# A gated scan with top-128 expert rows: loads and stores by units of both halves, plain transposes, a shared weighing

## The chip, the cores and the metric

The kernel runs on one core of one Trainium2 chip. The metric is device time in microseconds (us) of one execution. The kernel before takes 238.24 us in the median of three runs (237.73 to 239.63). The profile was taken in another execution of 240.62 us.

A core has five engines that work side by side: PE (matrix products and transposes; "PEld" is its loading of the stationary operand), DVE (VectorE), ACT (ScalarE), POOL (GpSimd) and SP, which here issues transfers. Sixteen DMA engines move data between HBM and the on-chip memory SBUF; PE writes its results into PSUM.

## What is computed

For each of 4 batches, a sequence of 6208 steps with 256 channels goes through a gated recurrence; then the 128 rows with the highest score get an expert's output added.

```python
sig = 1.0 / (1.0 + np.exp(-f_logit))
f = lower_bound + (1.0 - lower_bound) * sig
i = 1.0 - f
for t in range(S):
    h = f[:, t] * h + i[:, t] * x[:, t]
    y[:, t] = h
...
scores = np.einsum('bsd,d->bs', y, w_gate)
out = y.copy()
for b in range(B):
    top_idx = np.argpartition(-scores[b], capacity)[:capacity]
    xe = y[b, top_idx]
    h = np.maximum(xe @ w1, 0.0)
    ye = h @ w2
    g = 1.0 / (1.0 + np.exp(-scores[b, top_idx]))
    out[b, top_idx] = xe + g[:, None] * ye
```

B, S, D, F = 4, 6208, 256, 1024; capacity is 128; all data are float32.

## The kernel before

The host hands over x and f_logit transposed, as (batch, channel, step). The 256 channels are two halves of 128 partitions. A batch is cut into 24 blocks of 256 steps after a tail of 64 steps; blocks are grouped into units of four (UNITS; the last batch ends in units of 3 and 1). The work item is a half of a unit, `half(s)`, 50 in all, mostly 128 partitions by 1024 steps:

- `load_f` (L247) and `load_x` (L251): one transfer each on SP, 512 KB, a run of 4 KB per partition. There are 6 f buffers and 10 x buffers.
- `gate` on ACT (L261): sigmoid of -f_logit, that is (1 - sig). `forget` on ACT (L275): 1 - (1 - lower_bound) x gate, into a PSUM tile `gt` of which there are two. Where a unit has the tail, its 64 columns go through extra small instructions (L259, L274).
- `prepare` on POOL (L278), for the second half only: x times (1 - lower_bound). `weigh` on POOL (L282): x times gate. For the first two and the last two halves ("direct") DVE weighs in one instruction (L285).
- `scan` on DVE (L293): the recurrence, in place in x, multiply and add.
- `scores` on PE (L301): the scan times w_gate into one PSUM bank, by a matrix that puts each block on its own partition.
- `turn` on PE: transposes of 128 steps by 128 channels. The first half goes by a product with a diagonal matrix that also multiplies by (1 - lower_bound) (L307); the second half by a plain transpose (L309). Four go into one PSUM tile `pt`, of which there are two. `put` on ACT (L329) copies them to the row tile `ym`.
- `store` on SP (L332), once both halves of a unit are there: 1 MB, in runs of 2 rows = 2 KB. There are 10 `ym` buffers.

After a batch's last scores comes a search for the 128 rows (`choose`): `keep` copies the scores from PSUM (L388), `lanes` (L393) spreads them on PE over 32 partitions of a PSUM bank `acc`, `top` to `ranks` on DVE (L401 to L428) find and rank candidates, `pull` (L439) collects the row numbers, `flag` (L453) tells whether the short way was enough. `redo` on POOL (L456, L457) loads the flag and branches over a long loop that is the fallback. Then `experts`: `fetch` on POOL (L511) gathers the 128 rows from the output in HBM, PE transposes them (L516), multiplies by w1 (`up`, L536), ACT applies relu (L542), PE asks for the score again (L525) and multiplies by w2 (`down`, L545), DVE mixes (L549), and `scatter` on POOL (L552) writes the rows back. These steps use tiles of the same two `pt` slots, for the sum `py` also.

The order on each engine is fixed when the kernel is built: `Plan.run` takes every operation with an engine, a cost, a rank and what it waits for, and at each step starts the one that can start first, by rank where several can. Ranks are 10 per half; loads stand AHEAD = 30 before their half, transposes TURN = 10 and copies PUT = 60 after, stores STORE = 200 after, searches and experts FIND and EXPERT after the batch's end. The engines then follow that order, each waiting on semaphores.

Of the kernel before, what the change touches and what calls it, by code (L numbers as in the profile page):

```python
# [11 lines left out]
F16 = mybir.dt.float16  # L12
# [3 lines left out]
ALU = mybir.AluOpType  # L16
PSUM = bass.MemoryType.PSUM

P = 128
# [6 lines left out]
UNITS = [4, 4, 4, 4, 4, 4]  # L26
LAST_UNITS = [4, 4, 4, 4, 4, 3, 1]
FORM = ["pe", "pool"]
DIRECT = (2, 2)
XBUF, FBUF, YBUF = 10, 6, 10  # L30
AHEAD = 30.0
BACKLOG, STORE = 4.0, 200.0
EASED = 0
TURN, PUT, FIND, EXPERT = 10.0, 60.0, [20.0, 20.0, -20.0, -100.0], [150.0, 150.0, 300.0, 0.0]
# [111 lines left out]
def gated_scan_moe(tc, x, fl, lb, wg, w1, w2, outs, cap):  # L146
    nc = tc.nc
    v, a, pe, g = nc.vector, nc.scalar, nc.tensor, nc.gpsimd
    with ExitStack() as ctx:
# [5 lines left out]
        moe = ctx.enter_context(tc.tile_pool(name="moe", bufs=2))  # L155
# [18 lines left out]
        ones = const.tile([P, P], BF16, name="ones")
# [4 lines left out]
        g.iota(slot, pattern=[[1, P]], base=0, channel_multiplier=0,  # L179
               allow_small_or_imprecise_dtypes=True)  # L180
        slot1 = const.tile([P, 1], F32, name="slot1")
        g.iota(slot1, pattern=[[0, 1]], base=1, channel_multiplier=1,
               allow_small_or_imprecise_dtypes=True)
# [4 lines left out]
        vals = [const.tile([P, OWN, 3], BF16, name=f"vals{q}") for q in range(2)]  # L188
        for t in vals:
            g.memset(t, 1.0)  # L190
            v.tensor_copy(t[:, :, 1], lane.to_broadcast([P, OWN]))
# [7 lines left out]
        diag = const.tile([P, NH, P], F32, name="diag")  # L199
        for h in range(NH):  # L200
            if FORM[h] == "pe":
                v.tensor_scalar(diag[:, h], ident, ol[:, h : h + 1], None, ALU.mult)
                v.tensor_scalar(wgt[:, h : h + 1], wgt[:, h : h + 1], ol[:, h : h + 1], None, ALU.mult)

        wgr = const.tile([P, NH, NROW, CG], F32, name="wgr")
        g.memset(wgr, 0.0)
        for r in range(NROW):
            v.tensor_copy(wgr[:, :, r, r], wgt)

        units = []  # L210
        for b in range(B):
            blk0 = 0
            for nblk in LAST_UNITS if b == B - 1 else UNITS:
                tail = TAIL if blk0 == 0 else 0
                units.append((b, blk0, nblk, tail))
                blk0 += nblk
        halves = [(i, h) for i in range(len(units)) for h in range(NH)]
        N = len(halves)
        first_half = {}
        last_half = {}  # L220
        for s, (i, h) in enumerate(halves):
            first_half.setdefault(units[i][0], s)
            last_half[units[i][0]] = s
# [3 lines left out]
        xs, fs, gs, es, pts, yms, yts, wide = {}, {}, {}, {}, {}, {}, {}, {}  # L227
        chosen, fetched, carry = {}, {}, {}
# [4 lines left out]
        def half(s):  # L233
            i, h = halves[s]
# [4 lines left out]
            rows = slice(h * P, (h + 1) * P)  # L239
            p = 10.0 * s  # L240
            k = n / 1024
            direct = s < DIRECT[0] or s >= N - DIRECT[1]
            form = FORM[h]

            def load_f():
                fs[s] = fp.tile([P, n], F32, name="ft")
                nc.sync.dma_start(fs[s], fl[b, rows, t0 : t0 + n])  # L247

            def load_x():
                xs[s] = xp.tile([P, n], F32, name="xt")  # L250
                nc.sync.dma_start(xs[s], x[b, rows, t0 : t0 + n])  # L251

            def gate():
                if direct:
                    gs[s] = pf.tile([P, 4 * BLK], F32, name="gt")
                    a.activation(gs[s][:, :m], fs[s][:, tail:], ACTF.Sigmoid, scale=-1.0)
                    if tail:
                        es[s] = fp.tile([P, tail], F32, name="et", bufs=2)
                        a.activation(es[s], fs[s][:, :tail], ACTF.Sigmoid, scale=-1.0)  # L259
                else:  # L260
                    a.activation(fs[s], fs[s], ACTF.Sigmoid, scale=-1.0)  # L261

            def parts(main, rest):
                return ([(rest, 0, tail)] if tail else []) + [(main, tail, n)]

            def forget():
                if direct:
                    for f, c0, c1 in parts(gs[s][:, :m], es.get(s)):
                        a.activation(fs[s][:, c0:c1], f, ACTF.Identity, scale=nl[:, h : h + 1], bias=1.0)
                    return  # L270
                gs[s] = pf.tile([P, 4 * BLK], F32, name="gt")
                if tail:
                    es[s] = fp.tile([P, tail], F32, name="et", bufs=2)
                    a.activation(es[s], fs[s][:, :tail], ACTF.Identity, scale=nl[:, h : h + 1], bias=1.0)  # L274
                a.activation(gs[s][:, :m], fs[s][:, tail:], ACTF.Identity, scale=nl[:, h : h + 1], bias=1.0)  # L275

            def prepare():
                g.tensor_scalar(xs[s], xs[s], ol[:, h : h + 1], 1.0, ALU.mult, ALU.mult)  # L278

            def weigh():  # L280
                if not direct:
                    g.tensor_tensor(xs[s], xs[s], fs[s], ALU.mult)  # L282
                    return
                for f, c0, c1 in parts(gs[s][:, :m], es.get(s)):
                    v.scalar_tensor_tensor(xs[s][:, c0:c1], xs[s][:, c0:c1], 1.0 if form == "pe" else ol[:, h : h + 1], f, ALU.mult, ALU.mult)  # L285

            def scan():
                if direct:
                    todo = parts(fs[s][:, tail:], fs[s][:, :tail]) if tail else [(fs[s], 0, n)]
                else:  # L290
                    todo = parts(gs[s][:, :m], es.get(s))
                for f, c0, c1 in todo:
                    v.tensor_tensor_scan(xs[s][:, c0:c1], f, xs[s][:, c0:c1], carry[h] if blk0 or c0 else 0.0, ALU.mult, ALU.add)  # L293
                    carry[h] = xs[s][:, c1 - 1 : c1]

            def scores():
                for q in range(-1 if tail else 0, nblk):
                    j, r = place(blk0 + q)
                    c = tail + q * BLK
                    c0 = OFF if q < 0 else 0  # L300
                    pe.matmul(score[j * CG : (j + 1) * CG, b % 2, c0:], wgr[:, h, r], xs[s][:, c + c0 : c + BLK],  # L301
                              start=(h == 0 and blk0 + q < 3), stop=(h == NH - 1 and blk0 + q >= NBLK - 4),
                              skip_group_check=True)

            def flip(out, src):
                if form == "pe":
                    pe.matmul(out, src, diag[:, h], start=True, stop=True)  # L307
                else:
                    pe.transpose(out, src, ident)  # L309

            def turn(j0, j1):
                pts[s, j0] = ptp.tile([P, TP * P], F32, name="pt")
                blocks = xs[s][:, tail:].rearrange("p (k q c) -> p k c q", q=P, c=2)
                for j in range(j0, j1):
                    flip(pts[s, j0][:, (j - j0) * P : (j - j0 + 1) * P], blocks[:, j // 2, j % 2, :])

            def turn_tail():
                pts[s, "tail"] = ptp.tile([P, TP * P], F32, name="pt")
                flip(pts[s, "tail"][:tail, :P], xs[s][:, :tail])

            def put_tail():
                if h == 0:
                    yts[i] = yp.tile([tail, D], F32, name="yt", bufs=2)
                a.copy(yts[i][:, rows], pts[s, "tail"][:tail, :P])

            def put(j0, j1, copy=a.copy):
                if h == 0 and j0 == 0:
                    yms[i] = yp.tile([P, nblk * 2, D], F32, name="ym")
                copy(yms[i][:, j0:j1, rows], pts[s, j0][:, : (j1 - j0) * P].rearrange("p (j d) -> p j d", d=P))  # L329
# [278 lines left out]
```

## Time and profile before

| | |
|---|---|
| median of 3 runs | 238.24 us |
| the profiled execution | 240.62 us |
| its span, first to last instruction | 238.8 us |
| PE, DVE, ACT, POOL busy | 174.7, 153.0, 162.8, 145.7 us |
| bytes moved | 79.74 MB, mean 334 GB/s |
| mean granted PE clock | 0.895 of full |

In the profile's rows, `L282 POOL TENSOR_TENSOR xt<-xt,ft 128x1024 ... x38 | 89.3, 2359` reads: line 282, on POOL, writes xt from xt and ft, 38 times, 89.3 us in all, 2359 ns each; behind the next bar stands the idle time of the engine before them and what ended it. In the timeline, a row has start, length, engine, line, operation and count; in brackets the idle time before it and what ended that. A stage row has the busy time of PE, PEld, DVE, ACT and POOL with the number of instructions in brackets, then the granted PE clock, the busy share of the DMA engines and GB/s. "SPq" is SP's queue of transfers, "POOLq" POOL's instructions that are not counted as busy.

### The profile page before, as it was taken

Reading aid. Unit: us, or ns where it says so; the run is one execution under the profiler, and the core shown is the slowest. Engines: PE = TensorE matmul, PEld = TensorE weight load, DVE = VectorE, ACT = ScalarE, POOL = GpSimd, SP = SyncE. Lnnn points to the kernel's source line nnn. Section 1 sums busy time; section 2 is a strip of 40 time slices with the busy share of each in tenths; the row PEclk is TensorE's granted clock in tenths of the full one; section 3 lists DMA queues with packets and bytes.
Section 4 is the critical chain, followed back from the end, with each engine's and each line's share of the span. In section 5 each row is a group of like instructions: output and inputs, shape, how many; then the busy total and the mean of one; then the engine's idle time right before and its main releaser. Section 6 shows DMA issues by size and latency. Waiting matters only on the chain. (4 is left out here: it accounts for less than half of the span.)

```text
span 238.8 us, 3722 instructions
## 1 busy us (share of the span) xinstructions
PE 174.7 (73%) x1328; PEld 131.6 (55%) x1328; DVE 153.0 (64%) x180; ACT 162.8 (68%) x237; POOL 145.7 (61%) x94
## 2 busy tenths in 40 slices
PE   0095976669775688869637969987945999949892
PEld 0073555356553466528434867755732787729681
DVE  1798776899992776999545688899515660460000
ACT  4876999899989399967928694975946742611120
POOL 3099999899964978967079695883079703001101
PEclk9997699999999679967996779997997799976997
DMA  6999999999999999999999990999999997840000
GB/s 181 413 411 410 408 407 380 410 406 407 408 404 414 414 415 409 412 408 409 413 411 390 414 387 18 267 391 374 396 386 380 396 374 281 302 178 5 22 22 22
DMA packets 29418, 79.74 MB, mean 334 GB/s; under 512 B 2512, under 2 KB 4304, under 8 KB 29392
## 3 DMA queue, kind: packets, MB, share of 16 engines
q1 hardware_dynamic: 28720, 78.39, 85.2%
q0 software_dynamic: 384, 1.05, 1.2%
q8 instruction: 10, 0.16, 0.3%
q14 instruction: 16, 0.13, 0.1%
q10 hardware_dynamic: 288, 0.00, 0.1%
HBM read 53.48 MB, written 25.95 MB: 333 GB/s over the span
## 5 line engine op out<-in xcount | busy, mean ns | idle before, releaser
L282 POOL TENSOR_TENSOR xt<-xt,ft 128x1024 f32<-128x1024 f32 (+2 forms) x46 | 107.7, 2353 | 35.2 <-DMA xt<-x 15.9
L293 DVE TENSOR_TENSOR_SCAN xt<-gt,xt 128x1024 f32<-128x1024 f32 (+1 forms) x46 | 106.1, 2319 | 36.1 <-POOL xt L282 35.4
L307 PE MATMUL pt<-diag,xt 128*128 128x128 f32 (+1 forms) x392 | 64.4, 323 | 9.6 <-ACT ym L329 8.4
L329 ACT COPY ym<-pt 128x512 f32<-128x512 f32 (+1 forms) x98 | 53.8, 575 | 24.1 <-PE pt L307 13.3
L307 PEld LDWEIGHTS pt<-diag,xt 128*128 128x128 f32 (+1 forms) x392 | 57.4, 227 | 22.0 <-ACT ym L329 16.6
L275 ACT ACTIVATE gt<-ft,nl 128x1024 f32<-128x1024 f32 (+1 forms) x46 | 51.1, 1110 | 17.8 <-DVE xt L293 16.0
L301 PE MATMUL score<-xt,wgr 128*32 128x256 f32 (+1 forms) x400 | 36.9, 430 | 33.0 <-DVE xt L293 31.9
L261 ACT ACTIVATE ft<-ft 128x1024 f32<-128x1024 f32 (+2 forms) x46 | 48.8, 1061 | 0.4 <-DMA ft<-fl 0.3
L309 PE MATMUL pt<-ident,xt 128*128 128x128 f32 (+1 forms) x196 | 35.4, 320 | 5.7 <-ACT ym L329 5.6
L309 PEld LDWEIGHTS pt<-ident,xt 128*128 128x128 f32 (+1 forms) x196 | 28.5, 208 | 16.5 <-ACT ym L329 10.2
L278 POOL TENSOR_SCALAR xt<-xt,ol 128x1024 f32<-128x1024 f32 (+2 forms) x23 | 27.9, 1213 | 10.3 <-DMA out<-ym 9.7
L301 PEld LDWEIGHTS score<-xt,wgr 128*32 128x32 f32 x400 | 9.3, 115 | 42.8 <-DVE xt L293 27.0
L536 PE MATMUL pm<-xT,w1t 128*128 128x128 f32 x128 | 19.2, 316 | 2.4 <-ACT hT L542 1.9
L536 PEld LDWEIGHTS pm<-xT,w1t 128*128 128x128 f32 x128 | 17.9, 225 | 3.7 <-ACT hT L542 2.1
L552 POOL DMA_INDIRECT out<-res,idx x4 | 4.1, 1036 | 24.8 <-DVE res L549 24.8
L545 PE MATMUL pm<-w2t,hT 128*128 128x256 f32 x64 | 16.1, 394 | 1.0 <-ACT open L529 1.0
L511 POOL DMA_INDIRECT xe<-out,idx x4 | 4.2, 1044 | 19.1 <-issue 19.1
L549 DVE SCALAR_TENSOR_TENSOR res<-pm,open,xe 128x256 f32<-128x256 f32 x4 | 1.9, 478 | 20.9 <-PE pm L545 20.9
L542 ACT ACTIVATE hT<-pm 128x512 f32<-128x512 f32 x8 | 4.7, 592 | 13.6 <-PE pm L536 13.6
L545 PEld LDWEIGHTS pm<-w2t,hT 128*128 128x128 f32 x64 | 11.8, 194 | 3.9 <-ACT open L529 2.6
L428 DVE TENSOR_SCALAR_CACHE_REDUCE junk<-acc,mine 128x448 bf16<-128x448 f32 x16 | 10.9, 684 | 0.6
L293 DVE TENSOR_TENSOR_SCAN xt<-ft,xt 128x64 f32<-128x64 f32 (+2 forms) x6 | 8.0, 1335 | 0.1
(68 smaller groups left out, 72.9 us busy)
## 6 DMA issues: line engine op xcount, KB each, us to landing
out<-ym SPq DMA_DIRECT2D x23, 1024.0 KB, 10.0
ft<-fl SPq DMA_DIRECT2D x38, 512.0 KB, 9.6
xt<-x SPq DMA_DIRECT2D x38, 512.0 KB, 9.7
ft<-fl SPq DMA_DIRECT2D x8, 544.0 KB, 9.0
xt<-x SPq DMA_DIRECT2D x8, 544.0 KB, 8.6
w1t<-w SPq DMA_DIRECT2D x1, 1024.0 KB, 11.2
w2t<-w SPq DMA_DIRECT2D x1, 1024.0 KB, 13.7
ft<-fl SPq DMA_DIRECT2D x2, 384.0 KB, 9.3
```

The costliest lines, as they stand in the source:

```text
L261: a.activation(fs[s], fs[s], ACTF.Sigmoid, scale=-1.0)
L275: a.activation(gs[s][:, :m], fs[s][:, tail:], ACTF.Identity, scale=nl[:, h : h + 1], bias=1.0)
L278: g.tensor_scalar(xs[s], xs[s], ol[:, h : h + 1], 1.0, ALU.mult, ALU.mult)
L282: g.tensor_tensor(xs[s], xs[s], fs[s], ALU.mult)
L293: v.tensor_tensor_scan(xs[s][:, c0:c1], f, xs[s][:, c0:c1], carry[h] if blk0 or c0 else 0.0, ALU.mult, ALU.add)
L301: pe.matmul(score[j * CG : (j + 1) * CG, b % 2, c0:], wgr[:, h, r], xs[s][:, c + c0 : c + BLK], start=(h == 0 and blk0 + q < 3), stop=(h = ...
L307: pe.matmul(out, src, diag[:, h], start=True, stop=True)
L309: pe.transpose(out, src, ident)
L329: copy(yms[i][:, j0:j1, rows], pts[s, j0][:, : (j1 - j0) * P].rearrange("p (j d) -> p j d", d=P))
L428: v.tensor_scalar(junk, acc[:, :ROW], mine[:, k : k + 1], None, ALU.is_gt, ALU.add, accum_out=acc[:, A_RANK + k : A_RANK + k + 1])
L536: pe.matmul(st["pm", f // TP][:, c : c + P], w1t[:, h, f * P : (f + 1) * P], st["xT"][:, h], start=(h == 0), stop=(h == NH - 1))
L545: pe.matmul(st["py"][:, :D], st["hT"][:, f], w2t[:, f], start=(f == 0), stop=(f == NF - 1))
```

## The change

- The work item is a whole unit, `unit(i)`, with both halves in one tile. The host lays x and f_logit out unit by unit, so that a partition's part of a unit is one contiguous run: 8 KB for four blocks (half 0, then half 1). Loads are 1 MB each; there are 5 x and 3 f buffers. The weights w1 and w2 are laid out by partition too.
- Units are [1, 4, 4, 4, 4, 4, 3] in batch 0 and [3, 4, 4, 4, 4, 4, 1] in the others: 28 in all. Only the first and the last unit, of one block each, are direct.
- One sigmoid over both halves. `forget` and `scan` take the tail's columns with the rest, in one instruction.
- Both halves are multiplied on POOL by lower_bound - 1 (negative), so the scan subtracts; the diagonal matrix is gone and all transposes are plain. In the first half DVE weighs 256 of 1024 columns, as (forget - 1) x x, and POOL the others.
- Row p of a store's 128 partitions holds `cols` neighbouring rows of the output (8 for four blocks), a run of 8 KB; so a transpose reads every 8th step where it read every 2nd.
- In odd units, one of the four copies goes to DVE.
- The search's `top` and `ranks` are added to the plan as single steps; its tiles are single. A hint (`mark_branch_hint_location`) is placed on POOL before `redo`, and the branch's preferred fallthrough is named.
- The expert's sum `py` lies in the search bank `acc`, for batch 2 in a `gt` tile; `lanes` of the next search waits for the mix.
- The planner's constants change: AHEAD 60, PUT 30, FIND, EXPERT and several costs.

```diff
-UNITS = [4, 4, 4, 4, 4, 4]
-LAST_UNITS = [4, 4, 4, 4, 4, 3, 1]
-XBUF, FBUF, YBUF = 10, 6, 10
-AHEAD = 30.0
-TURN, PUT, FIND, EXPERT = 10.0, 60.0, [20.0, 20.0, -20.0, -100.0], [150.0, 150.0, 300.0, 0.0]
+UNITS = [[1, 4, 4, 4, 4, 4, 3], [3, 4, 4, 4, 4, 4, 1], [3, 4, 4, 4, 4, 4, 1], [3, 4, 4, 4, 4, 4, 1]]
+SHARE = 0.28
+XBUF, FBUF, YBUF = 5, 3, 10
+AHEAD, BACKLOG, STORE = 60.0, 4.0, 200.0
+TURN, PUT, FIND, EXPERT = 10.0, 30.0, [60.0, 60.0, 30.0, -100.0], [160.0, 160.0, 300.0, -100.0]
...
+            share = [n, n] if i in direct else [int(SHARE * m) // 32 * 32, 0]
+            span = slice((b * S + t0) * D, (b * S + t0 + n) * D)
+            def load(tiles, pool, name, src):
+                tiles[i] = pool.tile([P, NH, n], F32, name=name)
+                nc.sync.dma_start(tiles[i], src[span].rearrange("(p h c) -> p h c", p=P, h=NH))
             def gate():
+                a.activation(fs[i], fs[i], ACTF.Sigmoid, scale=-1.0)
...
+            def prepare(h):
+                c0 = share[h]
+                g.tensor_scalar(xs[i][:, h, c0:], xs[i][:, h, c0:], nl[:, h : h + 1], 1.0, ALU.mult, ALU.mult)
+            def weigh(h):
+                c0 = share[h]
+                g.tensor_tensor(xs[i][:, h, c0:], xs[i][:, h, c0:], fs[i][:, h, c0:], ALU.mult)
...
+                    v.scalar_tensor_tensor(xs[i][:, h, :c1], gs[i, h][:, :c1], 1.0, xs[i][:, h, :c1], ALU.subtract, ALU.mult)
+            def scan(h):
+                v.tensor_tensor_scan(xs[i][:, h], gs[i, h][:, :n], xs[i][:, h], carry[h] if blk0 else 0.0, ALU.mult,
+                                     ALU.subtract)
...
-            def flip(out, src):
-                if form == "pe":
-                    pe.matmul(out, src, diag[:, h], start=True, stop=True)
-                else:
-                    pe.transpose(out, src, ident)
+                for q, (h, c) in enumerate(part):
+                    pe.transpose(pts[key][:, q * P : (q + 1) * P], xs[i][:, h, tail + c :: cols], ident)
...
-                nc.sync.dma_start(outs[b][t0 + tail : t0 + n, :].rearrange("(k p c) d -> p k (c d)", p=P, c=2),
-                                  yms[i].rearrange("p (k c) d -> p k (c d)", c=2))
+                nc.sync.dma_start(outs[b][t0 + tail : t0 + n, :].rearrange("(p c) d -> p (c d)", p=P),
+                                  yms[i].rearrange("p c d -> p (c d)"))
...
+                eng = "dve" if part[0] == (1, TP) and i % 2 else "act"
...
+            def ready():
+                tc.mark_branch_hint_location(f"redo{b}", engines=[POOL])
             def redo():
                 val = g.value_load(st["flag"][0:1, 0:1])
-                with tc.If(val != 0):
+                with tc.If(val != 0, preferred_fallthrough_block=True, label=f"redo{b}"):
...
-            chain("pe", 0.8, lanes, extra=[("flag", b - 1)])
+            chain("pe", 0.8, lanes, extra=[("flag", b - 1), ("mix", b - 1 if b < B - 1 else b - 2)])
...
+            add("pool", 0.05, ready, p0, [("keep", b)], ("hint", b))
+            chain("pool", 1.5, redo, ("redo", b), extra=[("hint", b)])
...
-                st["py"] = psum()
+                st["py"] = acc if b != B - 2 else pf.tile([P, 4 * BLK], F32, name="py", tag="gt")
```

More of the change, by code (lines that the diff above doesn't have):

```diff
@@ L16 @@
 ALU = mybir.AluOpType
+AX = mybir.AxisListType
 PSUM = bass.MemoryType.PSUM
+POOL = mybir.EngineType.Pool
 P = 128
@@ L187, in gated_scan_moe @@
                    allow_small_or_imprecise_dtypes=True)
[L188 to L191, printed above, removed]
+        vals = const.tile([P, OWN, 3], BF16, name="vals")
+        g.memset(vals, 1.0)
+        v.tensor_copy(vals[:, :, 1], lane.to_broadcast([P, OWN]))
         order = const.tile([P, 4 * NROW], F32, name="order")
@@ L238, in half @@
             t0 = TAIL + blk0 * BLK - tail
-            rows = slice(h * P, (h + 1) * P)
-            p = 10.0 * s
+            cols = 2 * nblk
+            p = 20.0 * i
             k = n / 1024
[L242 to L251, printed above, removed]
@@ L311, in turn @@
[L311 to L315, printed above, removed]
+            def turn(key, part):
+                pts[key] = ptp.tile([P, TP * P], F32, name="pt")
+                for q, (h, c) in enumerate(part):
+                    pe.transpose(pts[key][:, q * P : (q + 1) * P], xs[i][:, h, tail + c :: cols], ident)
@@ L317, in turn_tail @@
             def turn_tail():
-                pts[s, "tail"] = ptp.tile([P, TP * P], F32, name="pt")
-                flip(pts[s, "tail"][:tail, :P], xs[s][:, :tail])
+                pts[i, "tail"] = ptp.tile([P, TP * P], F32, name="pt")
+                for h in range(NH):
+                    pe.transpose(pts[i, "tail"][:TAIL, h * P : (h + 1) * P], xs[i][:, h, :TAIL], ident)
             def put_tail():
-                if h == 0:
-                    yts[i] = yp.tile([tail, D], F32, name="yt", bufs=2)
@@ L324, in put_tail, with put @@
[L324 to L329, printed above, removed]
+                yts[i] = yp.tile([TAIL, D], F32, name="yt", bufs=2)
+                a.copy(yts[i], pts[i, "tail"][:TAIL, :D])
+            def put(key, part, eng):
+                if i not in yms:
+                    yms[i] = yp.tile([P, cols, D], F32, name="ym")
+                h, c0, w = part[0][0], part[0][1], len(part)
+                out = yms[i][:, c0 : c0 + w, h * P : (h + 1) * P]
+                src = pts[key][:, : w * P].rearrange("p (c d) -> p c d", d=P)
+                (v.tensor_copy if eng == "dve" else a.copy)(out, src)
@@ L366, in half @@
-            plan.alias(("turn", s), ("turnpart", me))
-            plan.alias(("put", s), ("putpart", me))
-            if h == NH - 1:
-                add("sp", 2.58 * k, store, 20.0 * i + STORE, [("put", s), ("put", s - 1), ("store", i - 1)], ("store", i), late=DONE)
+            add("sp", 2.5 * k, lambda: load(fs, fp, "ft", fin), p - AHEAD, [("weigh", i - FBUF, 1), ("here", i - FBUF, 1), ("forget", i - FBUF, 1), ("f", i - 1)], ("f", i), late=DONE)
+            add("sp", 2.5 * k, lambda: load(xs, xp, "xt", xin), p - AHEAD + 1, [("f", i), ("turn", i - XBUF), ("scores", i - XBUF + 1, 1)], ("x", i), late=DONE)
@@ new lines, in unit @@
+            add("act", 0.2 + 1.74 * k, gate, p, [("f", i)], ("gate", i))
+            for h in range(NH):
+                q = p + 10 * h
+                add("act", 0.2 + 0.91 * k, lambda h=h: forget(h), q + 1, [("gate", i), ("scan", i - 1, h)], ("forget", i, h))
+                w = share[h] / 1024
+                if w < k:
+                    add("pool", 0.1 + 1.1 * (k - w), lambda h=h: prepare(h), q, [("x", i)], ("ready", i, h))
+                    add("pool", 0.1 + 2.25 * (k - w), lambda h=h: weigh(h), q, [("gate", i), ("ready", i, h)], ("weigh", i, h))
+                if w:
+                    add("dve", 0.1 + 1.15 * w, lambda h=h: weigh_here(h), q, [("gate", i), None if i in direct else ("forget", i, h), ("x", i)], ("here", i, h))
+                add("dve", 0.14 + 2.2 * k, lambda h=h: scan(h), q, [("forget", i, h), ("weigh", i, h), ("here", i, h), ("scan", i - 1, h)], ("scan", i, h))
+                add("pe", 0.05 + 0.15 * nblk, lambda h=h: scores(h), q, [("scan", i, h), ("scores", i - (1 - h), 1 - h), ("keep", b - 2)], ("scores", i, h))
@@ new lines, in unit @@
+            todo, ends = [], []
+            for h in range(NH):
+                todo += [[(h, c) for c in range(c0, min(c0 + TP, cols))] for c0 in range(0, cols, TP)]
+            for part in todo:
+                h = part[0][0]
+                key = (i, *part[0])
+                eng = "dve" if part[0] == (1, TP) and i % 2 else "act"
+                add("pe", 0.175 * len(part), lambda key=key, part=part: turn(key, part), p + 10 * h + TURN,
+                    [("scores", i, h), ends[-1] if ends else None], ("turnpart", key), frees=("putpart", key))
+                add(eng, 0.16 + 0.105 * len(part), lambda key=key, part=part, eng=eng: put(key, part, eng), p + 10 * h + PUT,
+                    [("turnpart", key), ("store", i - YBUF)], ("putpart", key))
+                ends.append(("turnpart", key))
@@ new lines, in unit @@
+            if tail:
+                add("pe", 0.5, turn_tail, p + 10 + TURN, [("scores", i, 1), ends[-1]], ("turn", i), frees=("putpart", (i, "tail")))
+                add("act", 0.38, put_tail, p + 10 + PUT, [("turn", i)], ("putpart", (i, "tail")))
+            else:
+                plan.alias(("turn", i), ends[-1])
+            puts = [("putpart", e[1]) for e in ends] + ([("putpart", (i, "tail"))] if tail else [])
+            add("sp", 2.5 * k, store, p + STORE, [*puts, ("store", i - 1)], ("store", i), late=DONE)
@@ L386, in keep @@
             def keep():
-                wide[b] = new("wide", [P, BLK])
+                wide[b] = new("wide", [P, BLK], bufs=2)
                 a.copy(wide[b], score[:, b % 2])
@@ L573, in weights @@
         def weights():
-            nc.sync.dma_start(w1t, w1.rearrange("(h p) f -> p h f", p=P))
-            nc.sync.dma_start(w2t, w2.rearrange("(k p) d -> p k d", p=P))
-        for s in range(N):
-            half(s)
-        add("sp", 5.9, weights, WEIGHTS_AT, [], ("w",), late=DONE)
+            nc.sync.dma_start(w1t, w1.rearrange("(p h f) -> p h f", p=P, h=NH))
+            nc.sync.dma_start(w2t, w2.rearrange("(p k d) -> p k d", p=P, k=NF))
+        for i in range(N):
+            unit(i)
+        add("sp", 5.0, weights, WEIGHTS_AT, [], ("w",), late=DONE)
         for b in range(B):
```

264 lines of the change are left out of this document (100 added, 164 removed).

## The prediction

> **What bounds the kernel now.** I read the page first: busy times and slices, then the transfers.
>
> ```profile
> PE 174.7 (73%) x1328; PEld 131.6 (55%) x1328; DVE 153.0 (64%) x180; ACT 162.8 (68%) x237; POOL 145.7 (61%) x94
> ...
> DMA  6999999999999999999999990999999997840000
> GB/s 181 413 411 410 408 407 380 410 406 407 408 404 414 414 415 409 412 408 409 413 411 390 414 387 18 267 391 374 396 386 380 396 374 281 302 178 5 22 22 22
> ...
> HBM read 53.48 MB, written 25.95 MB: 333 GB/s over the span
> ```
>
> No engine is full. The DMA row is, from slice 2 to about slice 35 (208 us), with one hole in slice 25. After that it is nearly idle for 30 us. So there are two stages: transfers up to about 208 us, and a chain of small steps after the last load. I then looked at what one transfer costs, in a stretch of loads alone (12 to 28 us) and one of stores alone (188 to 200 us):
>
> ```profile
> DMA packets 1798, 6.55 MB, mean 409 GB/s; under 512 B 200, under 2 KB 200, under 8 KB 1798
> ...
> DMA packets 2348, 4.57 MB, mean 381 GB/s; under 512 B 92, under 2 KB 156, under 8 KB 2347
> ```
>
> The first has 1598 packets of 4 KB (a load's run is 1024 floats), the second about 2200 of 2 KB (a store's run is 512 floats). Both stretches are saturated, so the rate depends on the run. By stage:
>
> ```profile
> 0.00:188.00 188.00, 133.68 (x1051) 98.02 (x1052) 139.53 (x148) 147.57 (x205) 138.82 (x88) 0.89 0.98 379
> ...
> 143.00:149.00 6.00, 5.74 (x33) 4.49 (x32) 4.84 (x3) 2.84 (x5) 3.79 (x2) 0.91 0.06 26
> ```
>
> By 188 us, when the last loads are in, 379 x 188 = 71.3 MB have moved: 53 MB read, 18 MB written. The hole is 6 us at 26 GB/s. The waits of the SP queue and the timeline say why:
>
> ```profile
> SPq L251 <- PE pt L309: 24.9, 9, 9.9
> ...
> 146.11 1.99 PE L545 MATMUL pm<-w2t,hT 128*128 128x256 f32 x8 [0.26 <-ACT open L529]
> 147.94 0.63 PE L309 MATMUL pt<-ident,xt 128*128 128x128 f32 x4
> 148.60 0.33 SPq L251 DMA_DIRECT2D xt<-x  x1
> ```
>
> A load of x waited 9.9 us for its buffer, until a transpose that stood behind an expert on PE; every later transfer stood behind that load on SP.
>
> The chain at the end, from the last weighing:
>
> ```profile
> 189.07 1.81 POOL L282 TENSOR_TENSOR xt<-xt,ft 128x768 f32<-128x768 f32 x1 [1.38 <-ACT ft L261]
> ...
> 195.02 0.75 DVE L293 TENSOR_TENSOR_SCAN xt<-ft,xt 128x256 f32<-128x256 f32 x1
> ...
> 195.81 2.86 PE L545 MATMUL pm<-w2t,hT 128*128 128x256 f32 x12 [0.26 <-ACT open L529]
> ...
> 203.40 0.62 PE L301 MATMUL score<-xt,wgr 128*32 128x256 f32 x2
> ...
> 214.15 0.27 PE L439 MATMUL acc<-vals,hot 128*128 128x3 bf16 x4 [3.57 <-DVE hot L434]
> ...
> 215.61 0.15 DVE L453 CAST flag<-acc 1x1 int32<-1x1 f32 x1 [0.93 <-PE acc L449]
> ...
> 220.06 0.96 POOL L511 DMA_INDIRECT xe<-out,idx  x1 [18.14 <-issue]
> ...
> 222.23 2.86 PE L545 MATMUL pm<-w2t,hT 128*128 128x256 f32 x12 [0.26 <-ACT open L529]
> ...
> 224.92 0.38 PE L516 MATMUL pm<-ident,xe 128*128 128x128 f32 x2
> ...
> 234.95 0.98 POOL L552 DMA_INDIRECT out<-res,idx  x1 [8.00 <-DVE res L549]
> ```
>
> The last scan ends at 195.8, but PE comes to the last scores at 203.4, behind expert 1 and transposes; the search runs to 215.8, the last fetch starts at 220.1, PE is held by expert 2 until 225.1, and the last expert fills 225 to 235.
>
> **The change part by part.** *Runs of 8 KB.* Per engine of 16, 4096 B at 409 GB/s take 160 ns and 2048 B at 381 GB/s take 86 ns: 74 ns per 2 KB and 12 ns fixed. No row has 8 KB; on this line it takes 12 + 297 = 309 ns, or 425 GB/s. Up to 188 us that is 53/0.409 - 53/0.425 = 4.9 us for reads and 18/0.381 - 18/0.425 = 4.9 us for stores, 9.8 in all. The bounds are 0 (long runs are cut to the old packets) and 9.8; a loss is excluded, as the bytes are the same in longer contiguous runs. How much of it arrives depends on whether the engines keep up:
>
> ```profile
> L293 DVE TENSOR_TENSOR_SCAN xt<-gt,xt 128x1024 f32<-128x1024 f32 x44 | 102.6, 2343 | 36.1 <-POOL xt L282 35.4
> L282 POOL TENSOR_TENSOR xt<-xt,ft 128x1024 f32<-128x1024 f32 x38 | 89.3, 2359 | 31.6 <-DMA xt<-x 14.9 <-ACT ft L261 7.4 <-POOLq L457 6.7
> ...
> L329 ACT COPY ym<-pt 128x512 f32<-128x512 f32 x94 | 52.4, 584 | 21.7 <-PE pt L307 12.1 <-PE pt L309 8.6 <-issue 0.7
> L275 ACT ACTIVATE gt<-ft,nl 128x1024 f32<-128x1024 f32 x44 | 49.3, 1120 | 17.8 <-DVE xt L293 16.0 <-DVE idx L444 1.2
> L261 ACT ACTIVATE ft<-ft 128x1024 f32<-128x1024 f32 x38 | 40.4, 1063 | 0.4 <-DMA ft<-fl 0.3
> ...
> L278 POOL TENSOR_SCALAR xt<-xt,ol 128x1024 f32<-128x1024 f32 x19 | 23.3, 1228 | 10.1 <-DMA out<-ym 9.7 <-DVE xt L293 0.2
> ...
> L282 POOL TENSOR_TENSOR xt<-xt,ft 128x768 f32<-128x768 f32 x2 | 3.6, 1815 | 1.4 <-ACT ft L261 1.4
> ...
> L278 POOL TENSOR_SCALAR xt<-xt,ol 128x768 f32<-128x768 f32 x1 | 0.9, 902 | 0.0
> ...
> L285 DVE SCALAR_TENSOR_TENSOR xt<-xt,ol,gt 128x256 f32<-128x256 f32 x1 | 0.5, 457 | 0.0
> ```
>
> A unit of four blocks moves 3.15 MB: 7.9 us now, 7.4 after. POOL in that unit: now 1.23 + 2 x 2.36 = 5.9 us. After, both halves are prepared and VectorE takes 256 columns of the first: 0.90 + 1.82 + 1.23 + 2.36 = 6.3. ACT: one sigmoid of 2048 columns, at most 2 x 1.06 = 2.1; two forgets 2.2; four copies 2.3, one of them on VectorE in every second unit: 6.4 at most, down from 6.7. DVE: two scans 4.7, weighing 0.46, copies 0.3: 5.4. All stay under 7.4, POOL nearest; its fetches and scatters add 2 us a batch. I take 7 of the 9.8 us. The subtracting scan I cost at nothing: the row nearest is the same scan, and DVE has 2 us of cover a unit; without that cover each 0.1 us would cost 5.6 us over 56 scans.
>
> *Plain transposes.* Where PE ran at its full clock:
>
> ```profile
> 39.80 1.81 PE L307 MATMUL pt<-diag,xt 128*128 128x128 f32 x14
> 41.54 0.64 PE L301 MATMUL score<-xt,wgr 128*32 128x256 f32 x8
> 42.56 1.23 PE L309 MATMUL pt<-ident,xt 128*128 128x128 f32 x8 [0.38 <-ACT ym L329]
> ...
> 200.21 1.10 PE L307 MATMUL pt<-diag,xt 128*128 128x128 f32 x8
> ...
> 201.79 1.21 PE L307 MATMUL pt<-diag,xt 128*128 128x128 f32 x8
> ...
> 204.53 1.11 PE L307 MATMUL pt<-diag,xt 128*128 128x128 f32 x8
> ```
>
> A block through diag is two instructions of 129 ns, 258; a plain one 154. Per batch, 49 blocks of each become 98 plain ones: 20.2 to 15.1 us. Mid-stream that is hidden under the transfers. Ahead of the last scores and of the search's first step it is on the path: three groups of four blocks in diag form stand there (200.2, 201.8, 204.5), 12 x 0.104 = 1.2 us, which I take (lower bound 0). That holds if the new reading step costs nothing: a block was read two floats apart (8 B), and is now read eight apart (32 B) in a unit of four blocks. No row has that; bounds: 154 ns and, each read at half rate, 308.
> [...]
> I take 154, as the row at 8 B is nearest to it.
>
> *The expert's sum out of the transpose banks* (into the search bank, for batch 2 a gate tile). An expert no longer holds one of the two `pt` slots, so copies and transposes go on beside it. Bounds for the hole: 0 and 6 us. The order on PE still puts expert steps ahead of transposes, so I take 2. The price is a wait: the next search's `lanes` must wait for the mix of the expert before; behind it on PE stand all later transposes. Experts rank 160 and searches 200 or 170 after it, so the mix is earlier in the order; nothing added.
>
> *Branch hint on POOL.* First and last of four:
>
> ```profile
> L457 POOLq COMPARE_BRANCH  x4: 45/52/53, 69.5 to 216.2; - x4
> L457 POOLq EVENT_SEMAPHORE  x4: 17/17/17, 74.8 to 218.8; - x4
> ```
>
> POOL stands still 5.3 us after the first branch and 2.6 after the last. The first three are covered, as the DMA row stays full there (407 and 408 GB/s in the slices around 70 us). The last is on the path, but PE is late next: fetch at 220.06, 0.96, 2.8 to land
>
> ```profile
> xe<-out,idx POOLq DMA_INDIRECT x1, 2.8
> ```
>
> gives 223.8, and PE's flip comes at 224.9. So I take 0.9, bounds 0 and 2.6.
>
> *Against it:* the unit before the last has four blocks instead of three: POOL 6.3 against 0.90 + 2 x 1.82 = 4.5, 1.8 us later. Cover: PE reaches the last scores 7.6 us after the last scan; if that goes, 1.8. At the head, the first unit has one block in place of four, so the first gate starts earlier; but POOL's first work still waits for a whole unit's f and x, as now, so I count 0 (bounds: 1 us either way). The search in single steps lets copies (0.58) in between: 0.5.
>
> *Sum*, from the profiled execution's 240.62 us (span 238.8): -7 -2 -1.2 -0.9 +0.5 = -10.6, so 230.0. The median of the three runs, 238.24, stands 2.4 below that execution: **227.6**.
>
> **The rivals.** *Transfers gain little.* Loads stay at 409 (4 KB packets) and stores only reach 409: 18/0.381 - 18/0.409 = 3.2 us, seven tenths of it 2.2; the hole stays. -2.2 -1.2 -0.9 +0.5 = -3.8 from 238.2: **234**. For it: no packet here is longer than 4.25 KB. Against: the two rates differ by just what a fixed cost per packet gives. It also stands for a hint that does nothing, with POOL then at 6.3 + 7.3/6 (a stall of 5.3 and a fetch and a scatter of about 1 each, over six units) = 7.5 us a unit, above 7.4.
> [...]
>
> *PE becomes the bound (slower).* Per batch after: 15.1 of transposes, 100 x 0.08 of scores, 10.0 of expert (224.9 to 234.95) = 33.1 us, the search's small steps left out; transfers 79.4/4 MB / 425 = 46.7. The reserve, 13.6 over 98 blocks, is 139 ns: from 290 ns a block PE decides alone, and sooner with its clock below full. At 308 and the 0.89 granted up to 188 us it needs 48.2/0.89 = 54.2, 7.5 too much; half of that shows, as expert steps and transposes fill each other's waits: 15 in four batches, **243**. For it: PE is already the engine that makes the hole. Against: 308 is the far bound.
>
> *All of it arrives.* The full 9.8, the hole gone (6 in place of 2), and expert 2 no longer kept behind the search's `pull` (214.15): 1.5. 227.6 - 2.8 - 4 - 1.5 = **219**.
>
> **How the numbers follow.** Forecast 0.58, own range 222 to 233; little gain 0.20; all of it 0.12; PE 0.10. The range 218 to 239 takes in the first three with their unknown costs. A measurement here can tell about 1% (2.4 us) from no change. Faster: 0.56 + 0.12 + 0.13 = 0.81; same: 0.02 + 0.07 = 0.09; slower: 0.10.
>
> **What would show it.** Right: stretches of loads alone near 425 GB/s with packets of 8 KB; stores alone above 410; the last weighing on POOL near 182 us; plain transposes at 154 ns; under 1 us from the last branch to the fetch. Wrong: plain transposes above 290 ns at full clock with PE over 90% busy mid-stream; the hole in the DMA row as wide as before, or more of them; packets still at 4 KB.

## The result and the profile after

The changed kernel takes 229.52 us in the median of four runs (228.13 to 231.26), the kernel before 238.23 beside it: a ratio of 0.963, 95% interval 0.955 to 0.971. The forecast of 227.6 is 1.9 us below. The profiled execution took 229.47 us, its span is 227.3 us against 238.8, so 11.5 us of span are to be explained, 2.4 of them because the execution profiled before was that much longer than its median. Ratios leave out executions more than 1.5% above the fastest of their kernel, so they aren't quite the quotients of the medians, and of the profiles of share0 and old_ranks, which fell in such executions, only waits, busy times and order are read.

The page of the changed kernel:

```profile
PE 158.7 (70%) x1132; PEld 105.6 (46%) x1132; DVE 161.6 (71%) x210; ACT 152.7 (67%) x201; POOL 158.9 (70%) x127
...
DMA  6999999999999999999999999999999993810100
GB/s 185 427 425 425 421 418 416 418 424 424 412 428 424 416 417 394 423 424 418 422 427 413 418 387 426 417 365 342 430 418 368 411 423 125 346 69 3 49 0 23
```

The hole that stood in slice 25 of the old row is gone. A gap stands in slice 34 (125 GB/s), when the loads are in, and the transfers are nearly over with slice 35, which ends at 199 us; the old row still has 178 GB/s in slice 36, up to 215 us. The same by stage, first the kernel before, then the changed one (the first column is the stretch, the last two are DMA share and GB/s):

```profile
0.00:170.00 170.00, 122.09 (x972) 88.96 (x973) 131.69 (x144) 136.68 (x190) 125.88 (x80) 0.90 0.98 378
140.00:152.00 12.00, 11.06 (x67) 9.55 (x68) 10.65 (x7) 8.76 (x13) 8.61 (x6) 0.86 0.49 170
```

```profile
0.00:170.00 170.00, 117.49 (x856) 75.37 (x856) 131.61 (x156) 132.81 (x167) 142.55 (x116) 0.90 1.00 407
140.00:152.00 12.00, 6.13 (x38) 3.15 (x37) 6.47 (x8) 7.28 (x12) 9.58 (x8) 0.68 0.98 394
```

By 170 us, 29 GB/s x 170 us = 4.9 MB more have moved. Of these, (394 - 170) x 12 = 2.7 MB come from the 12 us around the hole. At about 410 GB/s that is 6.6 us of transfers for the hole and 5.4 for all the rest. How the loads come to wait no longer, in the waits of the SP queue (total us, times, longest):

```profile
SPq L224 <- ACT gt L231: 83.4, 24, 6.1
SPq L224 <- POOL xt L239: 39.6, 18, 6.1
...
SPq L224 <- PE pt L265: 3.6, 8, 0.8
```

Before, loads waited 24.9 us for L309, as shown, and for the product of the first half

```profile
SPq L251 <- PE pt L307: 18.3, 13, 5.2
```

43.2 us in all for transposes; now it is 3.6, never longer than 0.8. They wait for ACT and POOL instead, which is harmless as long as the DMA row stays full, as it does here up to 170 us (a share of 1.00).

The end, from the changed kernel's timeline:

```profile
180.29 2.37 POOL L239 TENSOR_TENSOR xt<-xt,ft 128x1024 f32<-128x1024 f32 x1
182.46 0.12 DVE L412 CAST flag<-acc 1x1 int32<-1x1 f32 x1
182.51 2.33 DVE L249 TENSOR_TENSOR_SCAN xt<-gt,xt 128x1024 f32<-128x1024 f32 x1
...
185.26 4.59 DVE L249 TENSOR_TENSOR_SCAN xt<-gt,xt 128x1024 f32<-128x1024 f32 x2
...
191.56 0.75 DVE L249 TENSOR_TENSOR_SCAN xt<-gt,xt 128x256 f32<-128x256 f32 x1
...
192.95 0.71 PE L265 MATMUL pt<-ident,xt 128*128 128x128 f32 x4 [0.76 <-DVE ym L282]
193.59 0.62 PE L258 MATMUL score<-xt,wgr 128*32 128x256 f32 x2
...
204.69 0.14 DVE L412 CAST flag<-acc 1x1 int32<-1x1 f32 x1 [0.41 <-PE acc L408]
...
208.96 0.95 POOL L477 DMA_INDIRECT xe<-out,idx  x1 [19.05 <-DVE res L515]
...
211.85 0.41 PE L482 MATMUL pm<-ident,xe 128*128 128x128 f32 x2 [3.97 <-DMA xe<-out,idx]
```

| mark | before | after | step's gain |
|---|---|---|---|
| last weighing ends | 190.88 | 182.66 | 8.2 |
| last scan ends | 195.77 | 192.31 | -4.8 |
| last scores start | 203.40 | 193.59 | 6.4 |
| flag starts | 215.61 | 204.69 | 1.1 |
| last fetch starts | 220.06 | 208.96 | 0.2 |
| end of the span | 238.8 | 227.3 | 0.4 |

The gain column is how much shorter the step from the mark above has become; it sums to 11.5. The gain of the stage of transfers is there at the last weighing; VectorE then gives 4.8 back, for it comes out of batch 2's search at 182.5 with three scans of 1024 steps and two of 256 still to do (8.4 us of scans); and PE no longer keeps the last scores waiting.

### The profile page after: what moved, and what is told of

It is laid out like the page before. It is cut to its first block, busy times and chain, and to the rows that moved or that the text cites. A ratio compares the mean times of both kernels' runs of the same rounds, so it can differ in the third digit from the quotient of the medians.

```text
span 227.3 us, 3277 instructions
## 1 busy us (share of the span) xinstructions
PE 158.7 (70%) x1132; PEld 105.6 (46%) x1132; DVE 161.6 (71%) x210; ACT 152.7 (67%) x201; POOL 158.9 (70%) x127
## 5 line engine op out<-in xcount | busy, mean ns | idle before, releaser
L249 DVE TENSOR_TENSOR_SCAN xt<-gt,xt 128x1024 f32<-128x1024 f32 (+4 forms) x56 | 114.4, 2051 | 23.1 <-POOL xt L239 20.2
L239 POOL TENSOR_TENSOR xt<-xt,ft 128x768 f32<-128x768 f32 (+6 forms) x52 | 100.0, 1923 | 4.6 <-POOLq L419 0.5
L265 PE MATMUL pt<-ident,xt 128*128 128x128 f32 x384 | 73.0, 335 | 9.5 <-ACT ym L282 8.1
L265 PEld LDWEIGHTS pt<-ident,xt 128*128 128x128 f32 x384 | 56.9, 204 | 38.5 <-ACT ym L282 22.2
L231 ACT ACTIVATE gt<-ft,nl 128x1024 f32<-128x1024 f32 (+4 forms) x56 | 56.3, 1008 | 12.9 <-DVE xt L249 4.9
L235 POOL TENSOR_SCALAR xt<-xt,nl 128x768 f32<-128x768 f32 (+6 forms) x52 | 49.4, 951 | 13.7 <-DMA xt<-x 12.5
L227 ACT ACTIVATE ft<-ft 128x2048 f32<-128x2048 f32 (+4 forms) x28 | 47.2, 1685 | 13.4 <-DMA ft<-fl 13.4
L246 DVE SCALAR_TENSOR_TENSOR xt<-gt,xt 128x256 f32<-128x256 f32 (+2 forms) x26 | 10.0, 383 | 7.1 <-ACT gt L231 7.1
L511 PE MATMUL acc<-w2t,hT 128*128 128x256 f32 x48 | 11.0, 381 | 0.4 <-ACT open L495 0.4
L511 PEld LDWEIGHTS acc<-w2t,hT 128*128 128x128 f32 x48 | 8.9, 190 | 1.6 <-ACT open L495 0.5
```

The lines of the kernel that those rows point to most:

```text
L227: a.activation(fs[i], fs[i], ACTF.Sigmoid, scale=-1.0)
L231: a.activation(gs[i, h][:, :n], fs[i][:, h], ACTF.Identity, scale=nl[:, h : h + 1], bias=1.0)
L235: g.tensor_scalar(xs[i][:, h, c0:], xs[i][:, h, c0:], nl[:, h : h + 1], 1.0, ALU.mult, ALU.mult)
L239: g.tensor_tensor(xs[i][:, h, c0:], xs[i][:, h, c0:], fs[i][:, h, c0:], ALU.mult)
L246: v.scalar_tensor_tensor(xs[i][:, h, :c1], gs[i, h][:, :c1], 1.0, xs[i][:, h, :c1], ALU.subtract, ALU.mult)
L249: v.tensor_tensor_scan(xs[i][:, h], gs[i, h][:, :n], xs[i][:, h], carry[h] if blk0 else 0.0, ALU.mult, ALU.subtract)
```

## The experiments

The question was which part carries the 8.7 us. The expectations name theories: A, the long runs do, as forecast; C, VectorE's share of the weighing does; R, the planner's ranks do. B and P, which also appear, say that the new order and the relief on PE do. On the three chips of the experiments the kernel before took 240.03, 240.11 and 239.01 us, so kernels are compared by their ratio to it; 0.01 is 2.4 us, and an interval is about 0.008 to each side, so about 0.011 for a difference of two. The changed kernel itself ran on the first of these chips only.

**The changed kernel again** (after_again).

> The changed kernel itself, unaltered, on the same chip as its variants: 228 to 231 us, to compare them with. Both theories expect the same.

Measured: 230.96 us, 0.962 [0.954, 0.969]. The result repeats, and this is the mark for the rest.

**Short runs** (runs_short both, loads_4k and stores_2k one each). The first two lines are runs_short and loads_4k, the next two runs_short and stores_2k:

```diff
-src[span].rearrange("(p h c) -> p h c", p=P, h=NH)
+src[span].rearrange("(h p c) -> p h c", p=P, h=NH)
...
-rearrange("(p c) d -> p (c d)", p=P)
+rearrange("(k p c) d -> p k (c d)", p=P, c=2)
```

> The changed kernel with its runs cut back: loads of 4 KB per partition and half, stores of 2 KB, transposes reading every second step again; all orders as in the changed kernel. Theory A (the run length brings most of the gain, since the transfers set the time of the last load): reads lose 4.9 us and stores up to 4.4 us until the last load, so the time rises from 229.5 by 6 to 9 us to 236 to 239, with loads alone back at 409 GB/s and stores at 381. Theory B (the gain comes from the new order and the relief on PE, the transfers are only a cover): at most 2 us more, 231.

> Only the loads are cut back to runs of 4 KB; stores keep 8 KB. Theory A: 53/0.409 - 53/0.425 = 4.9 us of transfer, of which 3.5 to 4.9 us arrive: 233 to 234.5. Theory B: under 1 us, 230.

> Only the stores are cut back to runs of 2 KB, and the transposes read every second step (8 B apart) in place of every eighth (32 B). Theory A: 3 to 4.5 us more, 232.5 to 234, and a plain transpose at full PE clock costs the same as at 32 B, 145 to 155 ns. Theory B: under 1 us more. A penalty for the wide step would show as transposes at least 20 ns faster than in the changed kernel.

Measured: 231.91, 231.96 and 231.49 us; 0.966 [0.958, 0.974], 0.967 [0.961, 0.973], 0.965 [0.959, 0.971]. Each is 0.8 to 1.2 us slower than the changed kernel by the ratios, less than the intervals. Between the two profiles it is 2.2 to 2.4: the last weighing of runs_short

```profile
182.50 2.36 POOL L239 TENSOR_TENSOR xt<-xt,ft 128x1024 f32<-128x1024 f32 x1
```

starts 2.2 us later, and its span is 229.7. But these two weren't taken side by side: beside them the kernel before took 238.23 and 240.03 us, which is most of that difference. Theory A, 6 to 9 us, falls. The rates tell why. Changed kernel, loads alone (12 to 28 us) and stores nearly alone (177 to 186, and the second half of that); then runs_short, loads of 4 KB alone (12 to 18) and stores of 2 KB nearly alone (179 to 188):

```profile
DMA packets 941, 6.79 MB, mean 424 GB/s; under 512 B 112, under 2 KB 112, under 8 KB 112
...
DMA packets 720, 3.72 MB, mean 413 GB/s; under 512 B 82, under 2 KB 146, under 8 KB 402
...
DMA packets 280, 1.90 MB, mean 422 GB/s; under 512 B 29, under 2 KB 49, under 8 KB 56
```

```profile
DMA packets 640, 2.47 MB, mean 411 GB/s; under 512 B 38, under 2 KB 38, under 8 KB 640
...
DMA packets 1894, 3.64 MB, mean 404 GB/s; under 512 B 86, under 2 KB 150, under 8 KB 1894
```

8 KB loads move at 424, a point from the forecast's 425, and 8 KB stores at 413 to 422: of the 402 packets under 8 KB in the longer stretch only 56 are in its second half. But 2 KB stores move at 404 here, not at 381. In the kernel before, the stretch from which I read 381 isn't even: its halves, from 188 to 194 and from 194 to 200 us, have

```profile
DMA packets 1196, 2.38 MB, mean 396 GB/s; under 512 B 34, under 2 KB 37, under 8 KB 1196
...
DMA packets 1152, 2.19 MB, mean 365 GB/s; under 512 B 58, under 2 KB 119, under 8 KB 1151
```

What slows the second I can't say (the 404 above holds as many packets between 512 B and 2 KB), but a mean over such a stretch is no price of a 2 KB run. By the new rates the whole term is 53/0.411 - 53/0.424 + 18/0.404 - 18/0.413 = 4.0 + 1.0 = 4.9 us, or 5.9 with 0.422, where I had 9.8, and 1.0 of it shows in the ratios; with their intervals it could be up to 3.7.

**Full products instead of plain transposes.** In diag the first half's blocks go through a product with the identity, at the new reading step of 32 B; in diag_2k at 8 B, with 2 KB stores, so its partner is stores_2k.

```diff
-pe.transpose(pts[key][:, q * P : (q + 1) * P], xs[i][:, h, tail + c :: cols], ident)
+if h == 0:
+    pe.matmul(out, blk, ident, start=True, stop=True)
+else:
+    pe.transpose(out, blk, ident)
```

> The first half's blocks go through a full product with the identity in place of a plain transpose: two instructions, 258 ns in place of 154 at full clock, 5 us of PE more in a batch; the planner's costs are left alone. Theory P: 3 us more or above, by later x buffers and later last scores. Theory C without P: only the blocks ahead of the last scores count, 0.5 to 1.5 us more.

> Stores of 2 KB with transposes that read every second step, as in the run stores_2k (231.5 us), and the first half through a full product with the identity: at this step two instructions of 129 ns, 258 a block as in the kernel before, in place of the 2 x 256 that the full product took at every eighth step. Theory P (PE's time for the blocks sets when x buffers and scores come): 5 us of PE more in a batch, 4 us or more in the time, 235 and above. Theory R (the new ranks, above all copies 30 in place of 60 after their half, bring the gain): at most 1.5 us more, 233.

Measured: diag 244.53 us, 1.024 [1.015, 1.033]; diag_2k 233.31 us, 0.975 [0.967, 0.983]. In diag PE is the bound. The stretch from 60 to 170 us in the changed kernel and in diag:

```profile
60.00:170.00 110.00, 82.36 (x620) 55.43 (x618) 89.43 (x108) 87.25 (x113) 95.27 (x70) 0.86 1.01 411
```

```profile
60.00:170.00 110.00, 101.68 (x677) 81.89 (x672) 86.53 (x103) 82.16 (x109) 86.17 (x65) 0.97 0.96 376
```

PE is busy 92% of it in diag, 75% in the changed kernel. Diag's timeline,

```profile
32.20 4.09 PE L267 MATMUL pt<-ident,xt 128*128 128x128 f32 x16
```

and plain transposes in the changed kernel at 32 B, and in stores_2k at 8 B:

```profile
42.68 1.15 PE L265 MATMUL pt<-ident,xt 128*128 128x128 f32 x8
```

```profile
32.62 1.23 PE L265 MATMUL pt<-ident,xt 128*128 128x128 f32 x8
```

An instruction of the full product takes 4.09/16 = 256 ns at 32 B, twice the 129 of 8 B in the kernel before; a block takes two of them. A plain transpose is one instruction a block, 1.15/8 = 144 ns at 32 B and 154 at 8 B. So the wide step doubles the product and costs the transpose nothing: with 8 KB stores the product makes the kernel slower than before. The rival "PE becomes the bound" (243) thus has its case in a kernel that keeps the product (244.5). At the old step the plain form is worth 0.975 - 0.965 = 0.010, 2.4 us, with intervals that overlap.

**Expert's sum back in a transpose bank** (py_in_pt).

```diff
-st["py"] = acc if b != B - 2 else pf.tile([P, 4 * BLK], F32, name="py", tag="gt")
+st["py"] = psum()
```

The plan then also counts the sum among the users of the two slots, and the sum of batch 2 no longer waits for the last unit's first scan.

> The expert's sum back in one of the two transpose slots, as in the kernel before; all else as changed. Theory P (the gain comes from x buffers that PE frees sooner): loads wait for transposes again, the hole in the transfers is back, 3 to 6 us more. Theory C without P (POOL paces and the plan hides PE): under 1.5 us more.

Measured: 232.06 us, 0.971 [0.962, 0.981]: 2.3 us slower by ratio, with intervals that overlap. The hole does not return; its stage has 406 GB/s:

```profile
140.00:152.00 12.00, 7.66 (x48) 4.56 (x45) 7.07 (x8) 7.76 (x12) 8.12 (x7) 0.78 0.99 406
```

The loads wait 11.9 us for transposes, between the 3.6 of the changed kernel and the 43.2 of the kernel before. So the sum's new place alone isn't what removed the hole.

**VectorE weighs nothing** (share0).

```diff
-SHARE = 0.28
+SHARE = 0.0
```

> VectorE weighs nothing outside the two direct units; POOL prepares and weighs both halves whole: (1.125 - 0.908) + (2.363 - 1.820) = 0.76 us more for each of 20 units of four blocks and about 0.5 for the others, 17 us in all. Theory C (POOL paces): 12 to 17 us more than the changed kernel. Theory A (transfers pace, POOL at 7.1 us a unit is still below 7.4): at most 3 us more.

Measured: 234.5 us, 0.981 [0.971, 0.991], 4.6 us slower. POOL's busy time rises from 158.9 to 176.6 us, yet only a quarter of these 17.7 us shows, though clear of the intervals. The scans' wait for POOL, in the changed kernel and in share0:

```profile
DVE xt L249 <- POOL xt L239: 20.2, 20, 3.5
```

```profile
DVE xt L249 <- POOL xt L239: 45.2, 34, 5.9
```

The scans wait longer for POOL, but POOL is not the only pace: C falls as the cause of the whole gain, and the share is worth about half of it.

**The hint inside a block of its own** (hint_block), so that it runs in the stream of the work.

```diff
-tc.mark_branch_hint_location(f"redo{b}", engines=[POOL])
+with tc.block():
+    tc.mark_branch_hint_location(f"redo{b}", engines=[POOL])
```

> The changed kernel with each branch hint placed where the plan puts it, in a small block of its own behind the batch's keep, in place of all four at the program's start. Theory C (POOL sets the pace up to the last weighing, so its standstills after the second and third branch, 5.1 and 4.2 us, count in full, and the 2.5 us after the last branch delay the last fetch): every branch then costs under 1 us, and the time falls by 7 to 11 us against the changed kernel. Theory A (the transfers set the pace, POOL's standstills are covered by buffers): only the last branch counts, 1 to 2 us.

Measured: 230.55 us (227.71 to 233.74), the kernel before 240.11 on the same chip; no difference from the changed kernel can be told. First and last of four branches, changed kernel and hint_block:

```profile
L419 POOLq COMPARE_BRANCH  x4: 53/56/70, 78.3 to 205.2; - x4
L419 POOLq EVENT_SEMAPHORE  x4: 17/17/17, 78.9 to 207.7; - x4
```

```profile
L420 POOLq COMPARE_BRANCH  x4: 49/60/64, 79.8 to 205.0; - x4
L420 POOLq EVENT_SEMAPHORE  x4: 17/17/17, 80.3 to 207.5; - x4
```

The first branch now takes 0.6 or 0.5 us instead of 5.3, the last 2.5 as ever, in both. The third is short in hint_block alone:

```profile
L420 POOLq COMPARE_BRANCH  x1: 62/62/62, 183.8 to 183.8; - x1
L420 POOLq EVENT_SEMAPHORE  x1: 17/17/17, 184.3 to 184.3; - x1
```

| POOL stands after the branch, us | first | second | third | last |
|---|---|---|---|---|
| kernel before | 5.3 | 5.4 | 5.3 | 2.6 |
| changed kernel | 0.6 | 5.1 | 4.2 | 2.5 |
| hint_block | 0.5 | 4.3 | 0.5 | 2.5 |

The third branch comes after the last weighing, so its 3.7 us had little to gain there. Theory C asked for every branch under 1 us; two of four are, so this run does not decide it. The hints themselves, in the changed kernel all in the first microsecond, in hint_block from 51.6 us on, the last 20 us ahead of its branch:

```profile
L579 POOLq BRANCH_PREFETCH_HINT  x4: 31/31/48, 0.7 to 0.9; - x4
```

```profile
L580 POOLq BRANCH_PREFETCH_HINT  x4: 38/40/41, 51.6 to 185.2; - x4
```

What POOL waits for in the stands of 2.5 to 5.4 us is not shown. Why the hints at the start go with one short branch, and the later ones with two, is open. So is the part that the named fallthrough has in it, which came in with the hints and which no run takes out.

**The old ranks** (old_ranks).

```diff
-AHEAD, BACKLOG, STORE = 60.0, 4.0, 200.0
-TURN, PUT, FIND, EXPERT = 10.0, 30.0, [60.0, 60.0, 30.0, -100.0], [160.0, 160.0, 300.0, -100.0]
+AHEAD, BACKLOG, STORE = 30.0, 4.0, 200.0
+TURN, PUT, FIND, EXPERT = 10.0, 60.0, [20.0, 20.0, -20.0, -100.0], [150.0, 150.0, 300.0, 0.0]
```

> The changed kernel with the planner's ranks of the kernel before (loads 30 ahead, copies 60 after, the old search and expert ranks). Theory R: 4 us more or above, 234.5 to 239, with loads waiting for transposes on SP again. Theory P: under 1.5 us more.

Measured: 237.19 us, 0.986 [0.978, 0.994]: 5.9 us slower, beyond the intervals and the largest part but for the product at the wide step. Its waits on SP and its stage of the old hole:

```profile
SPq L224 <- PE pt L265: 26.7, 14, 5.4
...
SPq L224 <- PE pt L270: 15.2, 3, 6.0
```

```profile
140.00:152.00 12.00, 7.41 (x48) 4.55 (x46) 5.29 (x7) 8.83 (x14) 5.03 (x6) 0.78 1.01 363
```

The loads wait 41.9 us for transposes again, as before the change, though the hole itself does not return. R holds for the changed kernel: there the ranks decide whether transposes free the x buffers in time. Which of the constants does it wasn't tried; PUT, which puts the copies out of the transposes' banks earlier, seems the likeliest, by its meaning alone. Nor was the kernel before run with the new ranks, so what they would be worth without the new units is not known.

**Four parts back at once, and the old kernel with plain transposes** (all_back: short runs, the product at 8 B, the sum in `pt`, old ranks; before_plain: one word in the kernel before).

```diff
-FORM = ["pe", "pool"]
+FORM = ["pool", "pool"]
```

> Short runs, the full product for the first half at every second step, the expert's sum in a transpose slot and the old ranks together; units of both halves, one sigmoid, subtracting scans and VectorE's part of the weighing stay. If these four parts carry the gain: 237 to 241. If what stays (units, one sigmoid, shared weighing) carries it: below 234.

> The kernel before with plain transposes for both halves (FORM pool, pool; the plan reckons with it) and POOL preparing both halves: 5 us of PE less in a batch, 28 us of POOL more in all. Theory P: faster than before by 3 us or more. If POOL is the nearer bound: not faster, up to 10 us slower.

Measured: all_back 247.48 us, 1.028 [1.018, 1.039]; before_plain 248.42 us, 1.037 [1.029, 1.044]. Both are slower than the kernel before. all_back's loads wait 48 us for transposes:

```profile
SPq L224 <- PE pt L270: 35.6, 13, 5.7
...
SPq L224 <- PE pt L275: 12.8, 3, 4.9
```

So the units of both halves, one sigmoid and the shared weighing, which all_back keeps, are no gain by themselves, at least under ranks that were set for the old units. Alone, its four parts cost 1.0 + 2.4 + 2.3 + 5.9 = 11.6 us, together 0.028 + 0.038 = 0.066, or 16; the difference is about the size of the intervals, so whether they hang together is open. In before_plain POOL prepares both halves without VectorE's share, and loads of f wait for it longer; the kernel before, then before_plain:

```profile
SPq L247 <- POOL xt L282: 38.1, 21, 5.7
```

```profile
SPq L247 <- POOL xt L282: 96.4, 35, 12.2
```

By themselves, plain transposes are no gain in the kernel before: what PE saves, POOL pays.

## Why the prediction was right, and where its sum was not

The time, the direction and several marks were right: loads at 424 GB/s (425), stores at 413 to 422 (above 410), the last weighing at 182.7 us (182). One mark was missed: from the last branch to the fetch it is 3.8 us, not under 1. The sum arrived there by terms that were off in both directions, so that it came within 1.9 us is in good part luck.

- *"I take 7 of the 9.8 us"* failed in both numbers. The runs are worth 1.0 us by the ratios, within intervals that reach to 3.7, out of 4.9 to 5.9 us of transfers in place of 9.8. The step that failed is the reading of 381 GB/s as the price of a 2 KB run. The fixed cost of 12 ns a packet came from it, though its 8 KB end happened to be right. The rival had the size of the gain (2.2 us) nearer, but not its reason: stores get past 409 (413 to 422 GB/s) and loads to 424; it was the old runs that were not so slow (2 KB stores move at 404 in runs_short, where I took 381).
- *The expert's sum, 2 of 6 us for the hole.* The hole went altogether, and stays away without the sum's new place, which is worth 2.3 us, unsure. What brings the loads' waits for transposes back is the old ranks, but the hole stays away there too (363 GB/s in its stage). What removed it is open.
- *"Nothing added" for the ranks* was the step that lacked a term. Of the planner's constants I costed only the wait that they might add. In the changed kernel they are worth 5.9 us, by the loads' waits. The other large step, from last scan to last scores, where expert steps and transposes stood on PE (7.6 us) and one group of transposes stands now (1.3), isn't theirs, nor that of the four parts together. In all_back the last scan ends at 204.4 us and the last scores start by 206.5:

```profile
201.24 3.19 DVE L249 TENSOR_TENSOR_SCAN xt<-gt,xt 128x1024 f32<-128x1024 f32 x2
...
205.81 1.05 PE L258 MATMUL score<-xt,wgr 128*32 128x256 f32 x4
```

  So it came with what all_back keeps, the new units and the order that the planner finds for them; no run takes these apart. I had costed 1.2 of these 6.4 us, as shorter transposes.
- *VectorE's share* stood in the sum only as a number that keeps POOL at 6.3 us a unit. POOL's rows bear it out:

```profile
L239 POOL TENSOR_TENSOR xt<-xt,ft 128x1024 f32<-128x1024 f32 x20 | 47.3, 2363 | 2.0 <-POOLq L419 0.5
...
L239 POOL TENSOR_TENSOR xt<-xt,ft 128x768 f32<-128x768 f32 x21 | 38.2, 1820 | 1.7
L235 POOL TENSOR_SCALAR xt<-xt,nl 128x1024 f32<-128x1024 f32 x20 | 22.5, 1125 | 0.0
L235 POOL TENSOR_SCALAR xt<-xt,nl 128x768 f32<-128x768 f32 x21 | 19.1, 908 | 12.5 <-DMA xt<-x 12.5
```

  2.36 + 1.82 + 1.13 + 0.91 = 6.2 us. Without the share 4.6 us are lost. The other side, VectorE later at the end (4.8 us more from weighing to scan), I did not see; I had counted 1.8 for the longer unit before the last, and on POOL. Subtracting in the scan costs nothing: 2345 ns against 2343.

```profile
L249 DVE TENSOR_TENSOR_SCAN xt<-gt,xt 128x1024 f32<-128x1024 f32 x40 | 93.5, 2345 | 13.9 <-POOL xt L239 12.4
```

- *Plain transposes, 1.2 us at 154 ns*: the price was right (144), the gain 2.4 at the old step, within the error; at the new step they are not a gain but a condition, worth 1.024 - 0.962 = 0.062, or 15 us. That the wide step is free for them was taken from the row at 8 B; no row showed it beforehand. It isn't free for the full product (256 against 129 ns). The far bound of 308 ns for a transpose, on which the rival "PE becomes the bound" stood, was an estimate, the 154 ns doubled; no run shows it.
- *The hint, 0.9 us*: nothing. The last branch is as slow as before (2.5 us against 2.6). PE now waits 3.97 us for the fetch, so the cover that limited this term to 0.9 is gone, and by an estimate from the short branches (2.5 - 0.5) a working hint could bring up to 2 us.
- *Search in single steps, +0.5*: the search is 1.1 us shorter, not longer.

The parts, taken out one by one, add up to more than the 8.7 us (1.0 + 2.4 + 2.3 + 5.9 + 4.6 = 16.2), and with four of them out the new units are slower than the kernel before; so the gain can't be shared out among the parts as a sum. No kernel tried is clearly faster than the changed one.

## What to carry to other kernels

A full DMA row says that transfers are the bound only after the order has been looked at: first ask what the loads wait for, and whether a rank or a priority can free their buffers sooner. Read a transfer's rate only from a stretch that keeps its rate when it is cut in two, before using it as a price. Cost every constant of a planner in a diff as if it were an instruction.

## What the runs showed of the hardware

- A full product that reads `xt` every 32 B takes 256 ns an instruction (diag) against 129 at 8 B (kernel before); a plain transpose takes 144 at 32 B (changed kernel) and 154 at 8 B (stores_2k).
- POOL stands still for 2.6 to 5.4 us at a branch in the kernel before. With hints at the program's start and a named fallthrough the first of four takes 0.6 (changed kernel), with later hints the first and third take 0.5 (hint_block); the last takes 2.5 in both.
- Loads move at 424 GB/s in 8 KB packets and at 411 in 4 KB, stores at 413 to 422 with 8 KB runs and at 404 with 2 KB (changed kernel and runs_short).
